# A ninth eighth in the first-stage buffer, another order of two interleaved transforms, and a half-size table of turns

## The chip, the cores and the metric

The kernel runs on one core of one Trainium2 chip. The time is device microseconds of one launch; the time before is the median of 10 runs, 204.54 us (203.83 to 204.83). One further execution was recorded by the hardware profiler; its times are microseconds from the start of its span.

The engines are named as in the profile: PE is TensorE's matmuls, PEld its weight loads, DVE is VectorE, ACT is ScalarE, POOL is GpSimd, SP is SyncE, which here only issues DMAs.

## The reference, cut to what matters

The sequence has 2048 positions, 512 channels and a batch of one; all tensors are bf16.

```python
def _A_ref(q, k, v, shift_k, ssm_k, ssm_D):
    # k_shift: four taps along the sequence
    for t in range(ks):
        k_shift = k_shift + k_pad[:, t:t + S, :] * shift_k[:, ks - 1 - t][None, None, :]
    kv = k_shift * v
    L = 2 * S
    kv_f = rfft2(kv_pad)          # along the sequence, zero padded to 4096
    kf_f = rfft2(kf_pad)          # ssm_k, the same
    y_f = kv_f * kf_f
    y = irfft2(y_f)[:S]
    y = y + kv * ssm_D
    return q * y

x = A_q
h = x + _A_ref(_layernorm(x), A_k, A_v, A_shift_k, A_ssm_k, A_ssm_D)
return h + _B_ref(_layernorm(h), B_w1, B_w2)      # B: relu(x @ w1) @ w2, 1376 wide
```

So there is a long convolution of kv with ssm_k, done by Fourier transforms, with a layer norm and a gate around it, and then an MLP.

## The kernel before

The transforms are written as matmuls with tables of sines and cosines. A transform of 4096 points is done in two stages: a first stage over short columns (`stage1`, 32 or 64 rows at a time against small bf16 tables) and a second stage (`stage2`, 128 by 128 tables `cc`, `cs` and `cn` in fp32r, one set for each of 32 odd frequencies k1). The tables are made on the chip: DVE computes turns as integers (`cs_turns`, `cc_turns`, `wrap`), ACT takes the sine (`table`, L193), and POOL makes the negated copy (`negated`, L250). The cosine's turns are the sine's plus a quarter (L222), wrapped (L189). Instructions are issued by hand in program order on each engine (`manual_schedule`), so the order of the Python code is the order on every queue; semaphores follow from which memory is written and read.

The stages that matter here, in order:

- **Loads and ssm_k to rows.** SP issues ssm_k, then k and v as four transposing loads each (L115 to L118). `to_rows` transposes ssm_k on PE, eight groups of four, and ACT or DVE copies each out of PSUM.
- **ssm_k's first stage with the taps** (L377 to L383), eight steps `gb`. In each, `taps` forms kv for a piece of the sequence: PE multiplies the shifted k by diagonal matrices (L369), and DVE multiplies the result by v (L372). Then `stage1` writes ssm_k's first-stage result to `a1` through two double banks of PSUM, evicted by ACT alone in even steps and by ACT and DVE in odd ones (`copy`, L259 on ACT, L261 on DVE). Steps 0 to 5 end with one `cc_part()`, which is one table on ACT: two for the sine's second part, then four for the cosine, from turns in `tcs`, which hold all 32 frequencies.
- **kv to rows** (L403): eight groups again, with evictions by DVE, ACT, DVE, DVE, ACT, DVE, ACT, DVE (L284 on DVE, L290 on ACT, two copies each).
- **The interleaved loop** (L410 to L421), eight steps `k4`. In each, ssm_k's second stage makes four frequencies, first the real part (evicted by DVE with ssm_D added, L418), then the imaginary part (evicted by ACT, L420). After both, one group of kv's first stage is made: two double banks, one evicted by ACT, the other by DVE (in groups 2 and 5 by DVE and ACT in halves). `a1` is one buffer of 64 KB a partition for both: a group of kv is written over the eighth that ssm_k's step has just read.
- **The product loop** (L475), 16 steps. kv's second stage (`u`), the complex product with ssm_k's spectrum (ACT copies a part of `u` to `usb`, L448; DVE and POOL multiply, L452, into `t`), and two steps later (`finish`) sums by matmul (`psy`, L462) and evictions into `kf`.
- **The inverse transform**, layer norm, gate and MLP, which take the rest of the span.

PSUM is handed out by `place`: `ring` is a list of tags, the first is taken and put at the back. Each tag is one double bank, and a tile waits until the tile before it on the same tag has been evicted. In the interleaved loop there are four tags (0 to 2 in the pool psF, 3 in psX); the order of tags there is 1, 3, 2, 0, so the real part always uses 1, the imaginary part 3 and kv's group 2 and 0. After the loop both pools are closed, and the product's `u` and `psy` tiles take their banks.

SBUF is full: on the left lie consts, `slotA` (a1, later `ax`), `vp` and `early`, whose place `kf` takes later; on the right lie the tables, `kvp` (k's first tiles), whose place `xfl`, then `prod` (the product loop's `t` and `usb`) and then `late` take.

Of the kernel before, what the change touches and what calls it, by code (L numbers as in the profile page):

```python
# [13 lines left out]
I32 = mybir.dt.int32  # L14
# [42 lines left out]
def kernel(  # L57
# [45 lines left out]
    kT = [(kvp if c < 2 else early).tile([P, DC, CH + 16], BF16, name=f"kT{c}") for c in range(4)]  # L103
# [79 lines left out]
    tcs = early.tile([P, 32, 64], I32, name="w_tc")  # L183
# [32 lines left out]
    dsc = early.tile([P, 2, 64], F32, name="dm_f")  # L216
    cs_turns(*cs[1])
    cc_parts = [(cs[1], tsn, dp) for dp in range(2)] + [(p, tcs, dp) for p in cc for dp in range(2)]

    def cc_turns(a):  # L220
        part = tcs[:, a:a + 16, :]
        nc.vector.tensor_single_scalar(out=part, in_=tsn[:, a:a + 16, :], scalar=2048.0, op=ALU.add)  # L222
        wrap(part, 8192)
# [47 lines left out]
    def bank2(name):  # L271
        return place([P, 2, 512], F32, name)
# [70 lines left out]
    cc_turns(16)  # L343
    _sin(dsc[:], t3[:], 64)
# [4 lines left out]
    a1 = slotA.tile([P, 64 * 256], F32R, tag="A", name="a1")  # L349

    def a1k_of(gb):
        return a1[:].rearrange("p (c j) -> p c j", j=256)[:, :, 32 * gb:32 * gb + 32]

    def a1k(c):
        return a1[:, 256 * c:256 * c + 256]

    def a1x_of(gb):
        return a1[:, 2048 * gb:2048 * gb + 2048].rearrange("p (c j) -> p c j", j=32)

    def a1x(c):  # L360
        return a1[:].rearrange("p (b c j) -> p b c j", b=8, j=32)[:, :, c, :]
# [15 lines left out]
    for gb in range(8):  # L377
        taps(gb // 2, gb % 2)
        stage1(kfl, a1k_of, gb, ("AA", "AD")[gb % 2], pairs=(gb == 2))
        if gb < 6:  # L380
            cc_part()
        if gb == 1:
            negated(22, 32)  # L383
# [25 lines left out]
    dcol = dtab[:].rearrange("p g r -> p (g r)").unsqueeze(2).to_broadcast([P, 256, 4])  # L409
    for k4 in range(8):  # L410
        ks = slice(4 * k4, 4 * k4 + 4)
        for s in range(2):
            ps = bank2("ps2k")
            for h in range(2):
                stage2(ps[:, h, :].rearrange("p (k j) -> p k j", k=2), a1k, 2 * k4 + h, s)
            pj = ps[:].rearrange("p b (k j) -> p j (b k)", k=2)
            if s == 0:
                nc.vector.tensor_tensor(out=kf[:, 0, :, ks], in0=pj, in1=dcol, op=ALU.add)  # L418
            else:
                nc.scalar.copy(out=kf[:, 1, :, ks], in_=pj)  # L420
        stage1(xfl, a1x_of, k4, ("A", "DA" if k4 in (2, 5) else "D"))  # L421
# [17 lines left out]
    def product(kp):  # L439
# [3 lines left out]
        for s in range(2):  # L443
            u = psu.tile([P, 2, 256], F32, tag=f"u{s}", name=f"u{s}")
            stage2(u[:].rearrange("p k (b j) -> p k b j", b=8), a1x, kp, s)
            usb = prod.tile([P, 256 - NJ, 2], F32, tag=f"usb{s}", name=f"usb{s}", bufs=2)
            uj = u[:].rearrange("p k j -> p j k")
            nc.scalar.copy(out=usb[:], in_=uj[:, po, :])  # L448
            t = prod.tile([P, 2, 256, 2], F32R, tag=f"t{s}", name=f"t{s}")
            for eng, in0, j in ((nc.vector, uj[:, dv, :], dv), (nc.gpsimd, usb[:], po)):  # L450
                n = j.stop - j.start
                eng.tensor_tensor(out=t[:, :, j, :], in0=in0.unsqueeze(1).to_broadcast([P, 2, n, 2]),  # L452
                                  in1=kfr[:, :, j, ks], op=ALU.mult)
            ts.append(t)
# [30 lines left out]
    ax = slotA.tile([P, P, 2, 64], F32R, tag="A", name="ax")  # L485
# [35 lines left out]
    bd = [late.tile([P, 2, 8, DC, 32], F32R, name="bd0")]  # L521
# [322 lines left out]
```

## Time and profile before

| what | value |
|---|---|
| median of 10 runs | 204.54 us |
| the profiled execution | 204.73 us |
| its span | 202.6 us |
| PE busy | 191.5 us (95%), 2337 matmuls |
| DVE busy | 145.0 us (72%) |
| ACT busy | 128.7 us (64%) |
| POOL busy | 85.5 us (42%) |
| granted TensorE clock | 1.00 over the span |

The span is what the profiler records from the first to the last instruction; the rest of the execution's time lies around it. Busy time of PE is modelled and overlaps from one matmul to the next, so a PE at 95% is not 95% of its peak; what counts is where it waits. A line of the timeline gives start, length, engine, line, operation, output and inputs, and in brackets how long the engine was idle before it and which instruction released it.

The stages lie in the span as follows: ssm_k's first stage with the taps until 35.4 us, kv to rows until 39.05, the interleaved loop until 60.4, the product loop until about 92.5, the inverse transform until 115, the MLP until the end.

### The profile page before, as it was taken

How to read it: one execution, taken by the hardware profiler on the slowest of the kernel's cores; microseconds unless marked ns; L12 is line 12 of the kernel's file. 1: busy time of each engine (PE TensorE's matmuls, PEld its weight loads, DVE VectorE, ACT ScalarE, POOL GpSimd, SP SyncE). 2: the span in 40 equal slices, each digit the busy share in tenths (PEclk: the TensorE clock that was granted, in tenths of full speed). 3: DMA queues.
4: the chain of work that ended last, by engine and by line, in shares of the span. 5: the costliest groups of instructions: out<-in, count | busy, mean ns of one | idle time of the engine just before them, and what ended most of it. 6: DMA issues, size and time to landing. Idle time of an engine off the chain costs nothing.

```text
span 202.6 us, 5574 instructions
## 1 busy us (share of the span) xinstructions
PE 191.5 (95%) x2337; PEld 135.3 (67%) x2337; DVE 145.0 (72%) x238; ACT 128.7 (64%) x199; POOL 85.5 (42%) x121
## 2 busy tenths in 40 slices
PE   7797979999997999999999999999999999999991
PEld 2473544999986989987998877545664556544451
DVE  7988767887877998988995698959477117662131
ACT  2668898778785888885979964924570583026300
POOL 7199995000006999995959384200120002002000
PEclk9999999999999999999999999999999999999999
DMA  6999992000000006819990979754481602160011
GB/s 185 332 218 146 180 161 58 3 5 3 3 3 5 0 3 184 263 42 227 234 234 15 110 92 186 140 104 106 88 155 50 110 0 52 32 97 29 0 52 52
DMA packets 48492, 20.06 MB, mean 99 GB/s; under 512 B 43380, under 2 KB 46932, under 8 KB 48468
## 3 DMA queue, kind: packets, MB, share of 16 engines
q1 hardware_dynamic: 47940, 19.71, 48.5%
q8 instruction: 18, 0.29, 0.6%
q10 hardware_dynamic: 528, 0.00, 0.1%
q14 instruction: 6, 0.05, 0.1%
HBM read 7.08 MB, written 2.10 MB: 45 GB/s over the span
## 4 chain that ended last, share of the span: by engine, by line
PE 69%; SPq 11%; DVE 8%; DMA 5%; ACT 3%; issue 1%; POOL 1%; ACTq 0%
PE ps1m L716 19%; PE ps2m L746 19%; PE psy L462 6%; PE ps2k L328 4%; SPq L118 4%; SPq L115 4%; PE ps2k L330 4%; PE u L328 4%; PE u L330 3%; DMA kT<-in_A_k_dram 3%; SPq L117 3%; PE pz L689 3%; PE ps L310 2%; PE pst L281 2%; PE pkv L369 2%; DVE st L547 2%
## 5 line engine op out<-in xcount | busy, mean ns | idle before, releaser
L731 ACT ACTIVATE h1T<-ps1m 128x512 bf16<-128x512 f32 (+1 forms) x44 | 25.7, 597 | 35.8 <-PE ps1m L716 35.7
L716 PE MATMUL ps1m<-xT,w 128*128 128x512 bf16 (+2 forms) x192 | 43.7, 365 | 0.4 <-DVE xT L662 0.4
L746 PE MATMUL ps2m<-w,h1T 128*128 128x512 bf16 (+3 forms) x187 | 40.8, 368 | 0.0
L689 PE MATMUL pz<-bd,ax 128*128 128x128 f32 x96 | 35.7, 410 | 0.0
L452 POOL TENSOR_TENSOR t<-usb,kf 128x320 fp32r<-128x320 f32 x32 | 28.2, 911 | 2.2 <-ACT usb L448 1.7
L452 DVE TENSOR_TENSOR t<-u,kf 128x704 fp32r<-128x704 f32 x32 | 26.7, 885 | 3.2 <-ACT usb L448 3.2
L750 DVE SCALAR_TENSOR_TENSOR o<-ps2m,rstd,xh 128x512 bf16<-128x512 f32 (+1 forms) x17 | 12.1, 717 | 22.5 <-PE ps2m L746 11.5
L746 PEld LDWEIGHTS <-h1T 128*128 128x128 bf16 (+1 forms) x187 | 16.2, 98 | 16.0
L553 POOL TENSOR_SCALAR rstd<-mv 128x4 f32<-128x4 f32 x8 | 2.5, 316 | 57.0 <-DVE mv L551 57.0
L259 ACT CAST a<-ps 128x1024 fp32r<-128x1024 f32 (+1 forms) x22 | 22.5, 1056 | 4.0 <-PE ps L310 3.9
L716 PEld LDWEIGHTS <-w 128*128 128x128 bf16 (+1 forms) x192 | 15.9, 100 | 12.1 <-DVE xT L662 0.5
L689 PEld LDWEIGHTS pz<-bd,ax 128*128 128x128 f32 x96 | 18.6, 193 | 7.6
L547 DVE BATCH_NORM_STATS2 st<-xh 128x6 f32<-128x512 bf16 x32 | 19.9, 679 | 0.4 <-DMA xh<-xT 0.4
L660 DVE TENSOR_TENSOR qT<-pz,qT 128x1024 bf16<-128x1024 f32 x8 | 9.8, 1220 | 13.5 <-PE pz L689 10.8
L259 ACT CAST kf<-psy 128x512 fp32r<-128x512 f32 x30 | 17.5, 644 | 1.9 <-PE psy L462 0.2
L537 ACT ACTIVATE bd<-ecw,nbias 32x512 fp32r<-32x512 int32 x24 | 17.3, 720 | 0.6
L369 PE MATMUL pkv<-kT,wdiag 128*128 128x512 bf16 x64 | 15.2, 380 | 2.2 <-POOL f_hi L247 1.1
L462 PE MATMUL psy<-t,ipos 128*128 128x512 f32 x48 | 16.0, 394 | 0.0
L261 DVE CAST a<-ps 128x1024 fp32r<-128x1024 f32 (+1 forms) x12 | 13.6, 1137 | 2.7 <-PE ps L310 2.6
L259 ACT CAST ax<-psi 128x1024 fp32r<-128x1024 f32 x13 | 12.3, 1040 | 3.7 <-PE psi L609 3.5
L372 DVE TENSOR_TENSOR sk<-pkv,vT 128x512 bf16<-128x512 f32 x16 | 10.7, 689 | 5.2 <-PE pkv L369 3.5
L609 PE MATMUL psi<-dre,kf 64*128 64x128 f32 x120 | 13.8, 275 | 0.1
(132 smaller groups left out, 399.2 us busy)
## 6 DMA issues: line engine op xcount, KB each, us to landing
sk<-in_A_ssm_k_dram SPq DMA_DIRECT2D x1, 2048.0 KB
xh<-in_A_q_dram SPq DMA_DIRECT2D x16, 128.0 KB
out_dram<-o SPq DMA_DIRECT2D x15, 128.0 KB
w<-in_B_w_dram SPq DMA_DIRECT2D x1, 1376.0 KB
w<-in_B_w_dram SPq DMA_DIRECT2D x1, 1280.0 KB
xh<-xT SPq DMA_TRANSPOSE x8
out_dram<-o SPq DMA_DIRECT2D x2, 64.0 KB
w<-in_B_w_dram SPq DMA_DIRECT2D x1, 96.0 KB
```

What stands on the lines that cost most here:

```text
L259: nc.scalar.copy(out=o, in_=i)
L328: nc.tensor.matmul(out=ps[:, kk, :], lhsT=at_k1(w_re, k1), rhs=a_in(2 * k1), start=True, stop=False, skip_group_check=True)
L330: nc.tensor.matmul(out=ps[:, kk, :], lhsT=at_k1(w_im, k1), rhs=a_in(2 * k1 + 1), start=False, stop=True, skip_group_check=True)
L369: nc.tensor.matmul(out=pss[i][:], lhsT=wdiag[:, 2 * h + i, j, :], rhs=kT[c][:, 2 * h + i, 16 - j:CH + 16 - j], start=(j == 0), stop=(j == ...
L452: eng.tensor_tensor(out=t[:, :, j, :], in0=in0.unsqueeze(1).to_broadcast([P, 2, n, 2]), in1=kfr[:, :, j, ks], op=ALU.mult)
L462: nc.tensor.matmul(out=psy[:], lhsT=m_[:], rhs=t_.rearrange("p j k -> p (j k)"), start=first, stop=not first)
L537: nc.scalar.activation(out=bd[h][rows, :, :, rg, :], in_=ecw[q % 2][rows, :, 256 * h:256 * h + 256].rearrange("p b (j n) -> p b j n", n=32 ...
L547: nc.vector.bn_stats(out=st[:, i, :], in_=src[:, i, :])
L689: nc.tensor.matmul(out=pz[:, il, :, a, :], lhsT=ax[:, 64 * rho + n2, :, :].rearrange("p d g -> p (d g)"), rhs=bd[h][:, rho, 4 * il + a, :, ...
L716: nc.tensor.matmul(out=ps1[fc][:fsz, 128 * ii.start:128 * ii.stop].rearrange("p (i t) -> p i t", t=P), lhsT=w1[:, c, fc * P:fc * P + fsz], ...
L731: nc.scalar.activation(out=h1T[:fsz, fc, :], in_=ps1[fc][:fsz, :], func=ACT.Relu)
L746: nc.tensor.matmul(out=ps2[:, 0:w], lhsT=h1T[:ksz, fc, i * P:(i + 1) * P], rhs=w2[:ksz, fc, ds], start=(fc == 0), stop=(fc == NFC - 1))
```

## The change

- `a1` gets nine eighths instead of eight and is allocated earlier. ssm_k's first-stage result lies in eighths 1 to 8, kv's groups go to eighths 0 to 7. Group 0 of kv has a place of its own, and group g may be written once ssm_k's step g-1 has read its eighth.
- The interleaved loop runs in another order. Step 0 is as before: real, imaginary, group 0. In step 1 group 1 stands between the real and the imaginary part, and group 2 after it. From step 2 on group k4+1 follows step k4, so that group 7 is made in step 6 and step 7 ends with ssm_k's imaginary part. The ring starts as 1, 0, 2, 3.
- The turns of the cosine, `tcs`, have room for 16 frequencies instead of 32. The second half is made in step 4 of ssm_k's first stage, in place of a table; the two tables that use it come in steps 5 and 6 instead of 4 and 5.
- The products' second buffer `t1` lies, for two steps out of three, in the ninth eighth of `a1`, which nothing reads any more; the pool keeps one buffer for the third.
- `bd0`, a table of the inverse transform, moves from `late` into the ninth eighth.
- k's third tile moves from `early` to `kvp`, and the sine `dsc` is taken in place.

```diff
--- before.py
+++ after.py
@@ -100,7 +100,7 @@
     draw = consts.tile([P, DC, 64], BF16, name="draw")
     vT = [vp.tile([P, DC, 512], BF16, name=f"vT{c}") for c in range(4)]
     CH = 512
-    kT = [(kvp if c < 2 else early).tile([P, DC, CH + 16], BF16, name=f"kT{c}") for c in range(4)]
+    kT = [(kvp if c < 3 else early).tile([P, DC, CH + 16], BF16, name=f"kT{c}") for c in range(4)]
     wdiag = kvp.tile([P, DC, KS, P], BF16, name="wdiag")
 
     idle = vT[3][:, 0, :]
@@ -180,7 +180,9 @@
         return t[:, k1 - a, :]
 
     tsn = early.tile([P, 32, 64], I32, name="w_ts")
-    tcs = early.tile([P, 32, 64], I32, name="w_tc")
+    tcs = early.tile([P, 16, 64], I32, name="w_tc")
+    EIGHTH = 64 * 32
+    a1 = slotA.tile([P, 9 * EIGHTH], F32R, tag="A", name="a1")
     ta = early.tile([P, 96], F32, name="w_ta")
     nc.vector.tensor_scalar(out=ta[:, 0:32], in0=r2[:, 0:32], scalar1=n2c[:], scalar2=4096.0, op0=ALU.mult, op1=ALU.add)
     nc.vector.tensor_scalar(out=ta[:, 32:96], in0=r2[:, 32:96], scalar1=n2c[:], scalar2=0.0, op0=ALU.mult, op1=ALU.add)
@@ -213,12 +215,12 @@
     t3 = early.tile([P, 2, 64], I32, name="dm_t")
     _turns(nc, t3[:, 0, :], r2[:, 32:96], n2s[:], 64, True)
     _turns(nc, t3[:, 1, :], r2[:, 32:96], n2s[:], 64, False)
-    dsc = early.tile([P, 2, 64], F32, name="dm_f")
+    dsc = t3[:].bitcast(F32)
     cs_turns(*cs[1])
-    cc_parts = [(cs[1], tsn, dp) for dp in range(2)] + [(p, tcs, dp) for p in cc for dp in range(2)]
+    cc_parts = [(cs[1], tsn, dp) for dp in range(2)] + [((0, p[1]), tcs, dp) for p in cc for dp in range(2)]
 
     def cc_turns(a):
-        part = tcs[:, a:a + 16, :]
+        part = tcs[:]
         nc.vector.tensor_single_scalar(out=part, in_=tsn[:, a:a + 16, :], scalar=2048.0, op=ALU.add)
         wrap(part, 8192)
 
@@ -340,25 +342,23 @@
 
     for q in range(8):
         to_rows(sk_word, q, kfl, "DADDADAD"[q])
-    cc_turns(16)
-    _sin(dsc[:], t3[:], 64)
+    _sin(dsc, t3[:], 64)
     dre = consts.tile([P, 2, 2, 64], F32R, name="dre")
     dim = consts.tile([P, 2, 2, 64], F32R, name="dim")
     nc.gpsimd.memset(dre[:].bitcast(F32), 0.0)
     nc.gpsimd.memset(dim[:].bitcast(F32), 0.0)
-    a1 = slotA.tile([P, 64 * 256], F32R, tag="A", name="a1")
 
     def a1k_of(gb):
-        return a1[:].rearrange("p (c j) -> p c j", j=256)[:, :, 32 * gb:32 * gb + 32]
+        return a1[:, EIGHTH:].rearrange("p (c j) -> p c j", j=256)[:, :, 32 * gb:32 * gb + 32]
 
     def a1k(c):
-        return a1[:, 256 * c:256 * c + 256]
+        return a1[:, EIGHTH + 256 * c:EIGHTH + 256 * c + 256]
 
     def a1x_of(gb):
-        return a1[:, 2048 * gb:2048 * gb + 2048].rearrange("p (c j) -> p c j", j=32)
+        return a1[:, EIGHTH * gb:EIGHTH * gb + EIGHTH].rearrange("p (c j) -> p c j", j=32)
 
     def a1x(c):
-        return a1[:].rearrange("p (b c j) -> p b c j", b=8, j=32)[:, :, c, :]
+        return a1[:, 0:8 * EIGHTH].rearrange("p (b c j) -> p b c j", b=8, j=32)[:, :, c, :]
 
 
     kvp2 = sk[:].rearrange("p c t -> p (c t)").rearrange("p (m c a e) -> p m c a e", m=32, c=DC, e=2)
@@ -377,7 +377,9 @@
     for gb in range(8):
         taps(gb // 2, gb % 2)
         stage1(kfl, a1k_of, gb, ("AA", "AD")[gb % 2], pairs=(gb == 2))
-        if gb < 6:
+        if gb == 4:
+            cc_turns(16)
+        elif gb < 7:
             cc_part()
         if gb == 1:
             negated(22, 32)
@@ -407,18 +409,29 @@
     slotB = pl.push("slotB")
     kf = slotB.tile([P, 2, 256, 32], F32R, tag="B", name="kf")
     dcol = dtab[:].rearrange("p g r -> p (g r)").unsqueeze(2).to_broadcast([P, 256, 4])
+
+    def spectrum_k(k4, s):
+        ks = slice(4 * k4, 4 * k4 + 4)
+        ps = bank2("ps2k")
+        for h in range(2):
+            stage2(ps[:, h, :].rearrange("p (k j) -> p k j", k=2), a1k, 2 * k4 + h, s)
+        pj = ps[:].rearrange("p b (k j) -> p j (b k)", k=2)
+        if s == 0:
+            nc.vector.tensor_tensor(out=kf[:, 0, :, ks], in0=pj, in1=dcol, op=ALU.add)
+        else:
+            nc.scalar.copy(out=kf[:, 1, :, ks], in_=pj)
+
+    def rows_kv(gb):
+        stage1(xfl, a1x_of, gb, ("A", "DA" if gb in (2, 5) else "D"))
+
+    ring[:] = [1, 0, 2, 3]
     for k4 in range(8):
-        ks = slice(4 * k4, 4 * k4 + 4)
-        for s in range(2):
-            ps = bank2("ps2k")
-            for h in range(2):
-                stage2(ps[:, h, :].rearrange("p (k j) -> p k j", k=2), a1k, 2 * k4 + h, s)
-            pj = ps[:].rearrange("p b (k j) -> p j (b k)", k=2)
-            if s == 0:
-                nc.vector.tensor_tensor(out=kf[:, 0, :, ks], in0=pj, in1=dcol, op=ALU.add)
-            else:
-                nc.scalar.copy(out=kf[:, 1, :, ks], in_=pj)
-        stage1(xfl, a1x_of, k4, ("A", "DA" if k4 in (2, 5) else "D"))
+        spectrum_k(k4, 0)
+        if k4 == 1:
+            rows_kv(1)
+        spectrum_k(k4, 1)
+        if k4 < 7:
+            rows_kv(k4 + 1 if k4 else 0)
     pl.pop("psX")
     pl.pop("psF")
     pl.pop("xfp")
@@ -446,7 +459,11 @@
             usb = prod.tile([P, 256 - NJ, 2], F32, tag=f"usb{s}", name=f"usb{s}", bufs=2)
             uj = u[:].rearrange("p k j -> p j k")
             nc.scalar.copy(out=usb[:], in_=uj[:, po, :])
-            t = prod.tile([P, 2, 256, 2], F32R, tag=f"t{s}", name=f"t{s}")
+            if s == 1 and kp % 3 < 2:
+                at = 8 * EIGHTH + 1024 * (kp % 3)
+                t = a1[:, at:at + 1024].rearrange("p (c j k) -> p c j k", c=2, k=2)
+            else:
+                t = prod.tile([P, 2, 256, 2], F32R, tag=f"t{s}", name=f"t{s}", bufs=3 - 2 * s)[:]
             for eng, in0, j in ((nc.vector, uj[:, dv, :], dv), (nc.gpsimd, usb[:], po)):
                 n = j.stop - j.start
                 eng.tensor_tensor(out=t[:, :, j, :], in0=in0.unsqueeze(1).to_broadcast([P, 2, n, 2]),
@@ -482,7 +499,8 @@
         if kp == 10:
             w1 = wp.tile([P, DC, DFF], BF16, tag="c2s0", name="w1")
             nc.sync.dma_start(out=w1[:], in_=B_w1.rearrange("(c p) f -> p c f", p=P))
-    ax = slotA.tile([P, P, 2, 64], F32R, tag="A", name="ax")
+    ax_bd = slotA.tile([P, 9 * EIGHTH], F32R, tag="A", name="ax")
+    ax = ax_bd[:, 0:8 * EIGHTH].rearrange("p (x d g) -> p x d g", x=P, d=2)
     load_x(2)
     load_x(3)
     pl.pop("psU")
@@ -518,7 +536,7 @@
     ecw = [late.tile([P, 2, 512], I32, name="ecw0"), wp.tile([P, 2, 512], I32, tag="c2s1", name="ecw1")]
     ecore0 = wp.tile([P, 2, 16, 32], F32R, tag="c2n0", name="ecore0")
     w2 = wp.tile([P, NFC, D], BF16, tag="c2n1", name="w2")
-    bd = [late.tile([P, 2, 8, DC, 32], F32R, name="bd0")]
+    bd = [ax_bd[:, 8 * EIGHTH:].rearrange("p (b j r n) -> p b j r n", b=2, j=8, r=DC)]
     act_pool = {0: late}
 
     def ec_turns(q):
```

## The prediction, made before the run

> **What bounds the kernel now.** I read three views in this order: the stretches of the span by engine, the chain of waits, and the timeline of each engine around the lines that the diff touches. The stretches (start:end, length, then busy us and instruction count of PE, PEld, DVE, ACT and POOL, the granted clock, DMA share, GB/s):
>
> ```profile
> 35.40:39.05 3.65, 3.65 (x32) 3.38 (x32) 3.50 (x5) 3.10 (x6) 0.00 (x0) 1.00 0.02 4
> 39.05:60.40 21.35, 21.35 (x642) 19.97 (x640) 17.65 (x17) 16.55 (x19) 0.00 (x0) 1.00 0.02 3
> 60.40:64.80 4.40, 2.89 (x28) 2.50 (x20) 2.95 (x4) 2.64 (x6) 2.47 (x4) 1.00 0.02 6
> 64.80:92.50 27.70, 27.68 (x172) 24.76 (x172) 25.50 (x31) 23.66 (x58) 26.53 (x31) 1.00 0.35 102
> ```
>
> TensorE (PE) sets the pace from 35.4 us on, at full clock. The interleaved loop (ssm_k's second step, kv's first) fills 21.35 of 21.35 us, the product loop 27.68 of 27.70. Between them lies one hole, and the timeline shows what it is made of (start, length, engine):
>
> ```profile
> 59.88 1.01 ACT L420 CAST kf<-ps2k 128x1024 fp32r<-128x1024 f32 x1 [0.70 <-PE ps2k L330]
> 60.79 1.08 ACT L259 CAST a<-ps 128x1024 fp32r<-128x1024 f32 x1
> 61.93 0.38 PE L328 MATMUL u<-a,c2c 128*128 128x256 f32 x1 [1.48 <-ACT a L259]
> 62.75 0.73 ACT L448 COPY usb<-u 128x160 f32<-128x160 f32 x2 [0.88 <-PE u L330]
> 63.08 1.69 DVE L452 TENSOR_TENSOR t<-u,kf 128x704 fp32r<-128x704 f32 x2 [1.29 <-ACT usb L448]
> ```
>
> PE idles 1.48 us because the first product reads what kv's last group (I write r7) has just left in PSUM, and its eviction on ACT queues behind ssm_k's. This is what the reordering aims at. Ahead of 35.4 us the chain of waits runs through the transposing loads on SP's queue: kT's last load is issued at 23.48 and lands at 30.10.
>
> **The change, part by part.** I write s0(k), s1(k) for the two halves of ssm_k's step k, r(g) for kv's group g.
>
> **1. The hole goes: -1.15.** Let F be the first matmul of s1(7), 58.74 in the PE timeline. Before, the first product on DVE starts at 63.08 = F+4.34. After, r7 is done one step earlier. ACT's copy of s1(7) starts F+1.14 (59.88), ACT takes its next work 0.91 later (60.79), so usb starts at F+2.05, and DVE follows it by 0.33 (63.08-62.75): F+2.38. PE's first product matmuls come at F+0.91 and usb could follow 0.82 after that (62.75-61.93), so ACT is what is late. That is 1.96 gained; but F now has r7 ahead of it, which costs PE 0.62 (a group, 41.08 to 41.72 less jitter) and 0.19 for the turn from wide to narrow matmuls (1.10 from s1 to a group, 0.91 from s0 to s1). Net 1.15, not 1.48: the hole is not filled but exchanged for ACT's 1.01 copy.
>
> **2. The cosine turns in halves push a table: +0.60.** With one half-size buffer, step 4 of ssm_k's first stage gives up its table to make the second half of the turns, and the last two tables (L193) move to steps 5 and 6. Nothing was behind step 6 on ACT before:
>
> ```profile
> 25.70 1.27 ACT L193 ACTIVATE c2c<-w_tc,hbi,hsc 128x1024 fp32r<-128x1024 int32 x1
> 26.84 2.06 ACT L259 CAST a<-ps 128x1024 fp32r<-128x1024 f32 x2
> ...
> 31.05 1.23 ACT L193 ACTIVATE c2c<-w_tc,hbi,hsc 128x1024 fp32r<-128x1024 int32 x1
> 32.73 2.04 ACT L259 CAST a<-ps 128x1024 fp32r<-128x1024 f32 x2 [0.44 <-PE ps L310]
> 35.17 1.13 ACT L259 CAST a<-ps 128x1024 fp32r<-128x1024 f32 x1 [0.41 <-PE ps L310]
> ...
> 36.36 0.96 PEld L281 LDWEIGHTS pst<-ident,sk 128*128 128x128 f32 x9 [0.16 <-ACT a L259]
> ...
> 36.36 3.62 DVE L284 TENSOR_SCALAR xfl<-pst 128x512 int32<-128x512 int32 x5
> ```
>
> The pair at 32.73 is step 6, the single at 35.17 step 7. A table delays the next copy by 1.14 (25.70 to 26.84), so with one between them step 7's copy starts at 34.65+1.14 = 35.79 instead of 35.17. The third kv transpose group (36.36) waits for exactly that PSUM bank: 35.17+1.13+0.06. So it moves 0.6, and with it DVE's dense row of five copies and s0(0), PE having no slack from there on. Step 4 without its table saves nothing: ACT idles 0.44 and 0.41 before steps 6 and 7 already. What is late next: s1(0) takes, by the new ring, the bank that DVE empties last (39.98 before), +0.04.
>
> **3. Two groups close together: +0.80.** The new order begins s0(0) s1(0) r0 s0(1) r1 s1(1) r2, over four double banks. r1 needs the bank of r0's half that ACT evicts, and ACT first copies s1(0):
>
> ```profile
> 41.31 1.01 ACT L420 CAST kf<-ps2k 128x1024 fp32r<-128x1024 f32 x1 [1.33 <-issue]
> 42.22 1.10 ACT L259 CAST a<-ps 128x1024 fp32r<-128x1024 f32 x1
> ```
>
> With r0's first matmul at R = 41.08 that bank is free at 43.32 = R+2.24 (+0.06 to the matmul); PE wants r1 at R+0.62+1.10 = R+1.72. Stall 0.55 (rounded down for jitter). Then r2 needs the bank of r1's ACT half: copy begins 0.80 after r1's first matmul (as DVE's at 41.92 does after 41.08), lasts 1.10, free 1.96 after; wanted at 1.72: 0.25. From r3 on a whole s0, s1 pair lies between groups and the rotation is the old one, where PE never waited.
>
> **4. The moved turns on DVE: 0 to +0.92, I take +0.15.** Two instructions (L222, L189) leave DVE at 13.52 and come back after step 4's products, at 27.89. Leaving gives nothing: PE waits for kT's load until 30.10. At 27.89 they stand ahead of step 5's two products (L372), which free the bank that PE's next taps need at 30.14. They are 0.69 each, but GpSimd is in the way:
>
> ```profile
> 12.35 2.04 POOL L238 TENSOR_TENSOR wdiag<-ident,wsh 128x512 bf16<-128x512 bf16 x2
> 14.33 1.99 POOL L247 COPY f_hi<-f_hi 32x64 bf16<-32x64 bf16 x4
> 25.64 3.45 POOL L250 TENSOR_SCALAR c2n<-c2s 128x1280 fp32r<-128x1280 f32 x1
> ...
> 13.52 1.42 DVE L222 TENSOR_SCALAR w_tc<-w_ts 128x1024 int32<-128x1024 int32 x1
> 14.97 0.69 DVE L189 TENSOR_SCALAR w_tc<-w_tc 128x1024 int32<-128x1024 int32 x1
> ```
>
> L222 alone took 0.69 at 8.21; here it took 1.42 and ended 0.55 after POOL's instruction did (14.39 to 14.94), while POOL's four copies then took 1.99 where the like four took 1.06. If POOL stays where it is, L250 ends at 29.09, L222 at 29.64, L189 at 30.33, the product after it at 31.0: PE is 0.92 late. But with L222 gone from 13.52, POOL's copies run 0.93 earlier and all behind them: L250 ends at 28.16, L222 at 28.71, L189 at 29.40, the product at 30.05, in time for 30.14. I take a value near this end, since the queue of POOL is unbroken from 12.35 to 29.
>
> The Trainium skill (SBUF — State Buffer, section "SBUF: two separate sides") says that VectorE's two-port modes and GpSimd take one shared port pair in turns, for a whole instruction. By it the turns are blocked until L250 ends, which is what I reckoned from the rows; the rows of 0.69 alone, without it, would make this term 0.
>
> **5. At nothing.** The products' buffers keep number, shape and strides (two of three in the ninth eighth): no new wait while the last s1 reads of that eighth precede them on PE. The sine table in place, kT's third tile in another pool and the offset of a1 change addresses only. bd0 moves into the ninth eighth; its memset (1.80, at 100.55 on POOL) comes after the last product matmul (92.73) as before, with 8 us until its first use at 110.32. No DMA is added or dropped; SP's x load waits for the last product and moves with it.
>
> **Sum.** -1.15+0.60+0.04+0.80+0.15 = +0.44 at the first product, and the product loop without slack hands it on whole; what waits later (x load, statistics, MLP) hangs from its end. The profiled execution took 204.73 (span 202.6 and 2.1 around it), 0.19 above the median: 205.17 in its terms, 204.54+0.44 = 205.0 in the median's. I forecast slightly slower. A difference under 0.2% (0.41 us) is about what a measurement of this kernel can't tell from no change, so this is on the edge.
>
> **Rivals.** (a) The late table is free: if transposes were not bound to that bank, part 2 falls away, -0.16 in all: 204.4. For it: ACT idles near there; against it: the wait at 36.36 names this very copy. (b) Faster: the close groups cost nothing, PE being fed through other banks while ACT catches up; +0.44-0.80 = -0.36: 204.2. It decides if ACT's copy of r0 ends within R+1.66; against it stands R+2.24. (c) POOL does not move up: part 4 costs 0.92: 205.75. Against: the unbroken queue. (d) The change doesn't do what it says: the product's PSUM pool waits for all evictions of the pool before it, s1(7)'s among them. Then PE starts at F+1.14+1.01+0.06, usb 0.82 later, DVE at F+3.36: gain 0.17 instead of 1.15: 206.0. The trace before can't tell, as there the same copy held data and bank.
>
> **How the numbers follow.** Forecast 0.58, of which slower 0.37, same 0.21 (its own range 204.7 to 205.4: jitter of 0.1 in four stalls, half of part 4); (a) 0.17, same 0.09, faster 0.08; (b) 0.14, faster 0.12, same 0.02; (c) 0.06 and (d) 0.05, slower. Faster 0.20, same 0.32, slower 0.48. The range 204.1 to 205.75 takes in (a), (b) and the upper end of part 4, and leaves out (d) and (a) with (b) together.
>
> **What would show it.** Part 1: the first u matmul follows s1(7) without a wait, and DVE's first product follows ACT's L420 copy by some 1.2 us. Part 2: a c2c table on ACT between step 6 and step 7, and the third transpose group later by 0.6. Part 3: two PE waits on ACT a L259 in the first three steps. Part 4: L222 near 27.9 lasting longer than 0.69. I am wrong if the first product on DVE is not between 63.2 and 63.9, or if the product loop or the MLP changes its length.

## The result, and the profile after

| what | before | after |
|---|---|---|
| median | 204.52 us (32 runs, 203.78 to 204.83) | 205.44 us (9 runs, 205.38 to 205.97) |
| ratio of after to before | | 1.0052, 95% interval 1.0042 to 1.0062 |
| profiled execution, its span | 204.73, 202.6 | 205.76, 204.0 |
| time outside the span, median of the runs | 2.14 | 1.78 |
| first matmul of the interleaved loop | 39.05 | 39.58 |
| first product on DVE | 63.08 | 64.27 |
| first pz matmul (inverse, second stage) | 110.69 | 111.72 |
| first gate instruction on DVE | 112.94 | 114.34 |
| first MLP matmul | 114.95 | 116.34 |

The kernel became slower by 0.92 us; 0.44 was forecast (205.0, within 204.1 to 205.75). Read down the table, the span's 1.39 is lost in three places: 0.53 before the interleaved loop, 0.66 in it and in the turn to the products, and 0.37 between pz and the gate; the product loop with the inverse transform gives 0.16 back. The time grew by less than the span, because what lies around the span is 0.36 shorter. It is shorter in every kernel that has the change (1.78 to 1.87 against 2.14); the runs do not show why.

The first view is PE's list of waits after the change (who waited for whom: us in all, times, longest); these are the lines that are new from 36 us on:

```profile
PE u L330 <- DVE kf L420: 0.6, 1, 0.6
PE pst L283 <- ACT a L261: 0.5, 1, 0.5
PE ps L312 <- ACT a L261: 0.3, 1, 0.3
PE ps2k L332 <- issue: 0.3, 1, 0.3
```

The old hole, 1.5 us at `u` for ACT's copy of kv's last group, is gone. Two of the four waits were forecast: `pst` (the late table) and `ps` (two groups close together). Two were not: the first product matmul waits for DVE, and in ssm_k's third step PE stands still for no semaphore at all ("issue"). The timeline shows the close groups and the stall in the third step:

```profile
43.45 0.20 PE L312 MATMUL ps<-f_hi,xfl 32*128 32x64 bf16 x2
43.98 0.20 PE L312 MATMUL ps<-f_hi,xfl 32*128 32x64 bf16 x2 [0.33 <-ACT a L261]
...
47.07 0.28 PE L330 MATMUL ps2k<-a,c2c 128*128 128x256 f32 x1
47.68 0.38 PE L332 MATMUL ps2k<-a,c2s 128*128 128x256 f32 x1 [0.33 <-issue]
```

Next the table on ACT between step 6 (the pair) and step 7 (the single copy), and PE behind it:

```profile
32.71 2.05 ACT L261 CAST a<-ps 128x1024 fp32r<-128x1024 f32 x2 [0.78 <-PE ps L312]
34.65 1.23 ACT L195 ACTIVATE c2c<-w_tc,hbi,hsc 128x1024 fp32r<-128x1024 int32 x1
35.78 1.05 ACT L261 CAST a<-ps 128x1024 fp32r<-128x1024 f32 x1
...
36.88 2.84 PE L283 MATMUL pst<-ident,sk 128*128 128x128 f32 x24 [0.46 <-ACT a L261]
```

From step 6's first copy to step 7's it is 3.07, against 2.44 before (32.73 to 35.17), and kv's third transpose group starts at 36.88 instead of 36.36. Last the turn to the products:

```profile
61.78 1.22 DVE L420 TENSOR_TENSOR kf<-ps2k,dtab 128x1024 fp32r<-128x1024 f32 x1
...
62.60 1.01 ACT L422 CAST kf<-ps2k 128x1024 fp32r<-128x1024 f32 x1 [0.64 <-PE ps2k L332]
63.15 0.36 PE L330 MATMUL u<-a,c2c 128*128 128x256 f32 x1 [0.58 <-DVE kf L420]
63.95 0.73 ACT L461 COPY usb<-u 128x160 f32<-128x160 f32 x2 [0.33 <-PE u L332]
64.27 0.89 DVE L469 TENSOR_TENSOR t<-u,kf 128x704 fp32r<-128x704 f32 x1 [1.27 <-ACT usb L461]
```

kv's group 7 was done long ago, but PE starts `u` only when DVE has evicted ssm_k's last real part (61.78 + 1.22). In the program `u` lies in other banks than that; what it waits for is the closing of the pool psF, of which the real part's bank is one. So ACT, free at 63.61 after the last imaginary part, idles 0.33 more, and DVE's first product comes 2.78 after the first matmul of s1(7) (61.49), not 2.38.

### The profile page after: what moved, and what is told of

It reads as the page before. It is cut to its first block, busy times and chain, and to the rows that moved or that the text cites. A ratio compares the mean times of both kernels' runs of the same rounds, so it can differ in the third digit from the quotient of the medians.

```text
span 204.0 us, 5565 instructions
## 1 busy us (share of the span) xinstructions
PE 193.3 (95%) x2337; PEld 136.0 (67%) x2337; DVE 144.5 (71%) x238; ACT 128.4 (63%) x199; POOL 85.6 (42%) x121
## 4 chain that ended last, share of the span: by engine, by line
PE 67%; DVE 11%; SPq 9%; DMA 5%; ACT 4%; issue 2%; POOL 1%; ACTq 0%; DVEq 0%
PE ps1m L734 19%; PE ps2m L764 19%; PE psy L479 6%; SPq L115 4%; PE u L330 4%; DMA vT<-in_A_v_dram 3%; PE ps2k L330 3%; PE u L332 3%; SPq L117 3%; PE pz L707 3%; PE ps2k L332 3%; PE ps L312 3%; SPq L118 2%; PE pst L283 2%; PE pkv L369 2%
## 5 line engine op out<-in xcount | busy, mean ns | idle before, releaser
L469 POOL TENSOR_TENSOR t<-usb,kf 128x320 fp32r<-128x320 f32 x21 | 19.2, 942 | 3.0 <-ACT usb L461 2.6
L469 DVE TENSOR_TENSOR t<-u,kf 128x704 fp32r<-128x704 f32 x21 | 18.2, 888 | 3.0 <-ACT usb L461 2.7
L678 DVE TENSOR_TENSOR qT<-pz,qT 128x1024 bf16<-128x1024 f32 x8 | 9.8, 1220 | 14.0 <-PE pz L707 10.8
L707 PE MATMUL pz<-ax 128*128 128x128 f32 x48 | 17.9, 410 | 0.0
L707 PE MATMUL pz<-bd,ax 128*128 128x128 f32 x48 | 17.8, 410 | 0.0
L627 PE MATMUL psi<-dim,kf 64*128 64x128 f32 x120 | 13.6, 270 | 0.0
L479 PE MATMUL psy<-t,ipos 128*128 128x512 f32 x37 | 13.5, 392 | 0.0
```

Of the source, the lines that this page charges most:

```text
L479: nc.tensor.matmul(out=psy[:], lhsT=m_[:], rhs=t_.rearrange("p j k -> p (j k)"), start=first, stop=not first)
L627: nc.tensor.matmul(out=banks[dp][:, 128 * i:128 * i + 128], lhsT=kf[halves[dp], c, 4 * m:4 * m + 4, :].rearrange("p r k -> p (r k)"), rhs= ...
L707: nc.tensor.matmul(out=pz[:, il, :, a, :], lhsT=ax[:, 64 * rho + n2, :, :].rearrange("p d g -> p (d g)"), rhs=bd[h][:, rho, 4 * il + a, :, ...
```

## The experiments

Each kernel was compared with the kernel before on the same chip; the medians of the kernel before there were 204.54 to 204.73. Times of different rows are compared through the ratio. Line numbers of variants can differ by up to five.

**The changed kernel once more.**

> The changed kernel once more, unaltered. Time 205.3 to 205.6. It tells which of the new idle stretches belong to the program. If the stall of 0.5 us in the middle of ssm_k's third step (a wait that the trace puts down to issue) and the extra 0.37 us between the product loop's end and the gate are properties of the program, both come again at the same instructions, within 0.1 us; if they are chance of one execution, at least one of them is gone and the span is shorter by its size. The late table (third group of kv's transposes at 36.9), the wait of kv's group 1 (0.5) and the wait of the first u matmul (0.58) hang from the order alone and must come again under every theory.

205.62 us, ratio 1.0036 (1.0021 to 1.0051). Every wait from kv's transposes on came again, at the same instruction and within 0.1: the stall without a semaphore at 47.63 (47.68 before), the gate 2.63 after pz (2.62). They belong to the program.

**The table in step 5 instead of after step 6.**

```diff
         if gb == 4:
             cc_turns(16)
-        elif gb < 7:
+        elif gb < 6:
             cc_part()
+            if gb == 5:
+                cc_part()
```

> The changed kernel with its last cosine table made in step 5 beside the one there, none after step 6. My theory (the late table holds ACT's copy of step 7, hence the bank of the third transpose group, hence everything): the third transpose group goes back from 36.9 to 36.4, the first matmul of the interleaved loop from 39.6 to 39.05, and the time falls by 0.5, to 204.9. Rival (the late table is covered, the changed kernel loses elsewhere): time unchanged at 205.4. Second rival (two tables in a row delay step 5's or step 6's evictions instead, by 1.1 less the idle time of 0.4 before each): the gain is smaller than 0.2 or turns into a loss.

205.15 us, ratio 1.0026 (1.0009 to 1.0043): 0.47 less than the changed kernel beside it by the medians. The two intervals overlap, so the size rests on the trace: the interleaved loop's first matmul is at 39.15, not 39.58. From step 6's copy to step 7's it is 2.45 again, and the transposes run without the gap. Two tables in a row in step 5 cost at most 0.13 (step 6's copy at 32.83, not 32.70), so the second rival is out.

**The kernel before with the late table alone.**

```diff
-        if gb < 6:
+        if gb < 7 and gb != 4:
             cc_part()
```

> The kernel before, with nothing changed but the place of its tables: none in step 4 of ssm_k's first stage, the last two in steps 5 and 6 (the turns are still made whole). My theory: the table after step 6 delays ACT's copy of step 7 by 0.6, the third group of kv's transposes with it, and the time by 0.5, to 205.1, although the old order of the interleaved loop and its hole before the first product are kept. Rival (the table is only late because the changed kernel's turns come late): no change, 204.6.

205.10 us beside 204.73, ratio 1.0023 (1.0001 to 1.0045): slower by 0.4, with an interval that just leaves out no change. On ACT (its timeline):

```profile
32.01 2.02 ACT L259 CAST a<-ps 128x1024 fp32r<-128x1024 f32 x2 [0.49 <-PE ps L310]
33.90 1.25 ACT L193 ACTIVATE c2c<-w_tc,hbi,hsc 128x1024 fp32r<-128x1024 int32 x1
35.27 1.16 ACT L259 CAST a<-ps 128x1024 fp32r<-128x1024 f32 x1
```

It is 3.26 from step 6 to step 7, but not by the table: that ended at 35.15, and the copy at 35.27 came when PE had step 7's matmuls done (35.29 by its signal). In this execution kT's last load landed early and step 6 with it (PE's taps for it at 29.03, not 30.14), while step 7's taps began at 32.70, behind DVE, which had waited for a load of v until 31.95. So this profile, with the old span of 202.6, does not show the table's cost; the profiled execution took 204.70, the least of its twelve, and the 0.4 is shown by the medians alone.

**The third double bank in a pool of its own.**

```diff
+    psum2 = pl.push("psG", space=PSUM)
...
-    places = [psum] * 3
+    places = [psum, psum, psum2]
...
+    pl.pop("psG")
     pl.pop("psF")
```

> The changed kernel with the third double bank of the interleaved loop in a PSUM pool of its own, closed one pool apart from the two others, so that the first u matmul waits for kv's group 7 alone and not for DVE's eviction of ssm_k's last real part. My theory (closing a pool makes the first tile behind it wait for the last eviction of the whole pool): the wait of 0.58 before the first u matmul goes, the first copy into usb follows ACT's copy of the last imaginary part, DVE's first product starts 0.4 earlier, time 205.0. Rival (ACT's copy is what is late anyway): the wait goes and the time stays at 205.4.

205.29 us, ratio 1.0023 (1.0008 to 1.0038), 0.33 less. The timeline:

```profile
62.15 0.28 PE L331 MATMUL u<-a,c2c 128*128 128x256 f32 x1
...
62.34 1.02 ACT L423 CAST kf<-ps2k 128x1024 fp32r<-128x1024 f32 x1 [0.69 <-PE ps2k L333]
...
63.26 0.82 ACT L463 COPY usb<-u 128x160 f32<-128x160 f32 x3
...
63.59 0.89 DVE L471 TENSOR_TENSOR t<-u,kf 128x704 fp32r<-128x704 f32 x1 [0.90 <-ACT usb L463]
```

`u` follows s1(7) without a gap, ACT goes straight from `kf` to `usb`, and DVE starts 2.39 after s1(7)'s first matmul (61.20): the 2.38 of the prediction. Closing the pool as a whole cost 0.40.

**Groups further apart.** On top of the split pool:

```diff
-    ring[:] = [1, 0, 2, 3]
+    ring[:] = [1, 0, 3, 2]
     for k4 in range(8):
         spectrum_k(k4, 0)
-        if k4 == 1:
-            rows_kv(1)
+        if k4 < 2:
+            rows_kv(k4)
         spectrum_k(k4, 1)
-        if k4 < 7:
-            rows_kv(k4 + 1 if k4 else 0)
+        if 0 < k4 < 7:
+            rows_kv(k4 + 1)
```

> The one before with the order of the first three steps also changed: kv's groups 0, 1 and 2 each get one half of ssm_k's step more between them (real, group 0, imaginary, real, group 1, imaginary, group 2), and the ring starts 1, 0, 3, 2. My theory (groups 1 and 2 wait for the bank that ACT evicts, since two groups follow each other with one half between them): group 1 has no wait, group 2 one of 0.25 or less, 0.5 less than the kernel with the split pool alone: 204.5. Rival (the close groups cost nothing, as PE is late for another reason): same time as the kernel with the split pool alone.

204.59 us, ratio 0.9995 (0.9977 to 1.0012): 0.7 less than the split alone, and the kernel before's time. The bank wait of group 1 is gone from PE's list; the stall without a semaphore grew:

```profile
PE ps2k L333 <- issue: 0.5, 1, 0.5
PE pst L284 <- ACT a L262: 0.5, 1, 0.5
PE u L331 <- DVE t L471: 0.3, 1, 0.3
```

In the profile 0.35 lies ahead of the loop (its first matmul at 39.21, not 39.56; GpSimd was through with L252 before DVE's turns began). From there to DVE's first product it is only 0.16 shorter, 23.87 against 24.03: what the bank waits gave back went to the stall, which grew from 0.35 between two matmuls to 0.79. So the loop alone does not explain the 0.7 of the medians; nothing that was edited lies ahead of the loop, and the rest stays open.

**Every group between the two halves of its step.** On top of the split pool, the real part's bank now being the one in psG:

```diff
-    places = [psum, psum, psum2]
+    places = [psum, psum2, psum]
...
-    ring[:] = [1, 0, 2, 3]
+    ring[:] = [1, 2, 0, 3]
     for k4 in range(8):
         spectrum_k(k4, 0)
-        if k4 == 1:
-            rows_kv(1)
+        rows_kv(k4)
         spectrum_k(k4, 1)
-        if k4 < 7:
-            rows_kv(k4 + 1 if k4 else 0)
```

> The changed kernel with the split pool, and with every group of kv between the real and the imaginary part of its own step, so that two halves of ssm_k's step lie between any two groups. Against the spread order (where three groups of 64 narrow matmuls still follow within 5 us and PE idles 0.65 in ssm_k's third step without a semaphore). Theory A (PE runs out of instructions where narrow matmuls are dense): that idle time goes, the turn to the products costs 0.1 more, time 204.1. Theory B (the idle time belongs to that place, whatever comes before): it stays, time 204.6 to 204.7.

205.33 us, ratio 1.0027 (1.0010 to 1.0043). A miss twice over. Its list of waits:

```profile
PE u L331 <- DVE a L264: 0.8, 1, 0.8
PE ps L313 <- issue: 0.5, 1, 0.5
```

I had put the turn to the products at 0.1 and overlooked that DVE then evicts s0(7) and group 7 one after the other (60.41 and 61.55, 1.22 each). And the stall did not go with the dense groups: it is there, in the middle of a group of kv. Theory A in that form fell, but so did B, since it is another place in the work. What the two have in common shows when PE's instructions up to the stall are counted. From the view of stretches, first the changed kernel, then this one (start:end, length, busy us and count of PE and PEld):

```profile
0.00:47.60 47.60, 42.79 (x859) 27.12 (x859) 37.22 (x67) 34.35 (x41) 27.21 (x55) 1.00 0.73 137
```

```profile
0.00:47.15 47.15, 41.91 (x859) 26.90 (x859) 37.27 (x67) 33.73 (x40) 27.18 (x55) 1.00 0.73 138
```

859 weight loads in both, and 859 in the spread order too (0 to 46.85). PE stops (from 47.07 to 47.68 after the change, from 46.53 to 47.21 here) at one point of its stream of instructions, whatever work stands there. The DMA of the same stretches fits: nothing of the kernel is transferred there, yet there is traffic (last column, GB/s). Before:

```profile
43.00:44.40 1.40, 1.40 (x73) 1.23 (x71) 1.28 (x2) 0.87 (x2) 0.00 (x0) 1.00 0.08 18
44.40:46.40 2.00, 2.00 (x20) 1.91 (x16) 1.86 (x2) 1.46 (x2) 0.00 (x0) 1.00 0.00 0
```

After:

```profile
43.00:44.40 1.40, 1.07 (x63) 0.83 (x62) 1.40 (x2) 0.93 (x1) 0.00 (x0) 1.00 0.00 0
44.40:46.40 2.00, 1.99 (x101) 1.72 (x88) 1.57 (x2) 1.65 (x2) 0.00 (x0) 1.00 0.05 12
46.40:48.00 1.60, 1.27 (x28) 1.03 (x16) 0.69 (x1) 1.60 (x3) 0.00 (x0) 1.00 0.00 0
```

18 GB/s over 1.40 us are 25 KB, as are 12 over 2.00; the page lists two queues of kind "instruction" with 18 and 6 packets (0.29 and 0.05 MB, so 16 KB and 8 KB each). The piece that came between 43.0 and 44.4 before comes after 44.4 now. The fit is a loose one: after the change the traffic is over by 46.40, and PE stops only after 47.07.

**The same work in more instructions.** The warming matmuls at the start, ahead of everything, were cut smaller, in the changed kernel alone and in the best one (below):

```diff
-    for _ in range(22):
-        nc.tensor.matmul(out=warm[:], lhsT=idle[:, 0:P], rhs=idle, start=True, stop=True)
+    for _ in range(44):
+        nc.tensor.matmul(out=warm[:, 0:256], lhsT=idle[:, 0:P], rhs=idle[:, 0:256], start=True, stop=True)
```

> The changed kernel with nothing altered but its warming matmuls: 44 of 256 columns in place of 22 of 512, so that 22 matmuls and weight loads more stand ahead in PE's stream. If the idle time in ssm_k's third step (0.45 to 0.5 beyond the usual spacing) is a matter of where PE's stream of instructions is cut, it goes as it did in the kernel with the spread order, the stretch from the first matmul of the interleaved loop to DVE's first product shrinks from 24.6 to 24.15, and the time falls to 205.0 to 205.1; the bank waits of group 1 and of the first u matmul stay. If the reordered loop brings the idle time with it wherever the stream is cut, both stay at 24.6 and 205.5.

> The one before, with the warming matmuls at the start as 44 of 256 columns in place of 22 of 512: the same work and time on PE, but 22 matmuls and as many weight loads more in its stream of instructions. Theory A (PE's idle time in the third step is its supply of instructions: it stood at the 859th matmul in three different orders): the idle time moves by some 22 matmuls in the work, or changes its length, or is gone (then 203.2 to 203.4). Theory B (it belongs to the place in the work): again 0.65 at the sixth matmul of ssm_k's third real part, same time as the one before.

> The same with 88 warming matmuls of 128 columns: 66 matmuls and weight loads more ahead. Theory A: the idle time moves by some 66 matmuls, to before or into ssm_k's second step, or is gone (203.2 to 203.4). Theory B: no change against the one with 22.

The kernels with 44 and 88 pieces in the best one took 203.84 (ratio 0.9961, 0.9944 to 0.9978) and 203.69 (0.9967, 0.9947 to 0.9987). In all three the stall in the third step is gone. In two of them, though, PE now stands still earlier, as the lists from 10 to 75 us show, first the changed kernel with 44 pieces, then the best one with 88:

```profile
PE pkv L369 <- issue: 0.6, 1, 0.6
PE u L330 <- DVE kf L420: 0.5, 1, 0.5
...
PE pst L283 <- ACT a L261: 0.4, 1, 0.4
...
PE ps L312 <- ACT a L261: 0.3, 1, 0.3
```

```profile
PE ps L313 <- issue: 0.9, 1, 0.9
```

These stalls end at 19.21 and 29.63, and 221 and 477 weight loads stand ahead of them, against 859 ahead of the old one. With the matmuls and the waits counted that is 448, 960 and 1728 instructions: the places lie 512 and 768 apart, both multiples of 256. The kernel with the late table alone has a short stall at 960 as well (0.24 idle, at 31.40). So the stall depends on the place in PE's stream and not on the work that stands there, as theory A says.

From the loop's first matmul to DVE's first product it takes 24.00 (24.69 and 24.59 in the changed kernel's two profiles), in the best kernel 23.23 and 23.24 instead of 23.71, but there the loop begins later, at 39.42 and 39.22 instead of 39.03. That the stall is PE's supply of instructions is shown by where it stands. That it is worth its 0.5 in the time is not: the medians are 205.69 (ratio 1.0049, 1.0030 to 1.0069) for the changed kernel, and, for the best, 203.84 and 203.69 against 203.70. The profiled execution of the first was the fastest of its six, 204.64, the others took 205.27 to 205.99. Nor do the runs say why the piece comes later in the new order.

**GpSimd's zeroing and the gate.** First the zeroing of `bd1` moved to VectorE:

```diff
-    nc.gpsimd.memset(bd[1][:].bitcast(F32), 0.0)
+    nc.vector.memset(bd[1][:].bitcast(F32), 0.0)
```

> The changed kernel with the second table of the inverse transform (bd1) zeroed by VectorE instead of GpSimd; the rest unaltered. In the changed kernel and its four variants the first gate instruction on VectorE starts 2.62 after the first pz matmul, in the kernel before 2.25; GpSimd's zeroing ends within 0.03 of the moment at which PE is done, and the fourth sine into bd0 ends just as the gate starts. Theory A (VectorE has to wait behind GpSimd at the moment of the zeroing's end): the gate starts 2.25 after the first pz matmul, time 205.1. Theory B (the gate waits for the four sines, because bd0 now lies in one buffer with the inverse transform's operand): it stays at 2.62, time 205.5.

205.41 us, ratio 1.0040 (1.0019 to 1.0062). The gate starts right behind the zeroing, at 113.92, 2.46 after the first pz matmul, while the fourth sine into `bd0` runs until 114.06: it does not wait for the sines, so theory B fell. Theory A is not shown by it, since the zeroing (1.76 on DVE) itself ends after PE. And the MLP loses 0.4 (88.06 from its first matmul to the end, against 87.63), with another stall on issue at 117.35, ahead of which 3776 instructions stand on PE: 2048 more than ahead of the stall in the loop. Nothing is gained.

**All edits with the even order.**

> The changed kernel with all of it: both last tables in step 5, the split pool, every group of kv between the two parts of its own step, bd1 zeroed by VectorE. The costs that the runs before showed add up: 0.5 for the table, 0.4 for the pool, 0.55 for the close groups' bank waits, 0.5 for the idle time in the third step, 0.37 for the gate if it was GpSimd's doing. If all of them are terms of one sum, 203.2; without the last two, 204.0; if the gains overlap (one wait taking the other's place), 204.3 or more.

204.60 us, ratio 0.9995 (0.9977 to 1.0013). The gains did not add up: the even order gave back at `u`, and the MLP was longer by 0.4 as in the run before, with its stall on issue at the same place in PE's stream.

**The spread order, the table in step 5, and the zeroing split over both engines.**

```diff
-    nc.gpsimd.memset(bd[1][:].bitcast(F32), 0.0)
+    nc.gpsimd.memset(bd[1][:, 0].bitcast(F32), 0.0)
+    nc.vector.memset(bd[1][:, 1].bitcast(F32), 0.0)
```

> The spread order with the split pool, and with two edits more: both last tables in step 5, and bd1 zeroed half by GpSimd, half by VectorE, so that neither is at it when PE has finished the first half of pz. Against the spread kernel alone: 0.47 from the table, and the gate 2.25 after the first pz matmul in place of 2.62 if GpSimd's zeroing was what held VectorE (0.37, or 0.2 if something else is late next): 203.8 to 203.9. If the gate's delay is of another kind, 2.62 stays and the time is 204.1. PE's idle time of 0.65 in ssm_k's third step stays in any case.

203.70 us, ratio 0.9953 (0.9938 to 0.9968): with its two variants above the fastest of the study, and faster than both kernels. The gate, first before the change, then after it, then here (timelines of PE, POOL and DVE):

```profile
110.69 3.86 PE L677 MATMUL pz<-ecore,ax 32*128 32x256 f32 x128 [0.22 <-DVE ax L261]
...
111.15 1.80 POOL L652 MEMSET bd<- 128x2048 f32 x1
...
112.94 1.22 DVE L660 TENSOR_TENSOR qT<-pz,qT 128x1024 bf16<-128x1024 f32 x1 [1.86 <-ACT bd L537]
```

```profile
111.72 3.87 PE L695 MATMUL pz<-ecore,ax 32*128 32x256 f32 x128 [0.22 <-DVE ax L263]
...
112.19 1.80 POOL L670 MEMSET bd<- 128x2048 f32 x1
...
114.34 1.23 DVE L678 TENSOR_TENSOR qT<-pz,qT 128x1024 bf16<-128x1024 f32 x1 [2.22 <-ACT ax L555]
```

```profile
110.18 3.87 PE L700 MATMUL pz<-ecore,ax 32*128 32x256 f32 x128 [0.22 <-DVE ax L264]
...
110.65 0.95 POOL L674 MEMSET bd<- 128x1024 f32 x1
...
112.45 1.23 DVE L683 TENSOR_TENSOR qT<-pz,qT 128x1024 bf16<-128x1024 f32 x1 [0.80 <-ACT ax L559]
```

It is 2.27 instead of 2.62, so the edit removes the gate's 0.35. That GpSimd's zeroing is what held DVE does not follow. Before the change the same zeroing ended at the same moment, 2.26 after the first pz matmul (2.27 after the change), and the gate began there without a delay. The waits that DVE's queue carries out tell more (view of one line: count, shortest, middle and longest ns, first and last start). Before the change, after it, and here:

```profile
L660 DVEq EVENT_SEMAPHORE  x2: 21/1165/2309, 110.5 to 110.6; - x2
L662 DVEq EVENT_SEMAPHORE  x1: 21/21/21, 113.4 to 113.4; - x1
```

```profile
L678 DVEq EVENT_SEMAPHORE  x2: 21/1168/2315, 111.6 to 111.6; - x2
L680 DVEq EVENT_SEMAPHORE  x1: 21/21/21, 114.4 to 114.4; - x1
```

```profile
L683 DVEq EVENT_SEMAPHORE  x2: 21/981/1941, 110.0 to 110.5; - x2
```

The two waits of L660, L678 and L683 stand ahead of the gate, the one of L662 and L680 behind it. Before the change the wait behind the gate comes 0.41 after the gate's start. After the change it comes 0.04 after it, and it is the gate that comes 0.40 after the wait for PE is over (113.94). Here the second wait comes 0.42 after the first, where the other two kernels have 0.05. So one step of DVE's queue is some 0.4 late in each kernel, and counted along the queue it is the same one: after the change one more instruction stands ahead of the gate than before, and with a zeroing on DVE two more. All fourteen profiles have it there, 0.40 to 0.42 late. Before the change it fell behind the gate, after the change on the gate, and here on a wait for PE that lasts until 112.40 anyway. By these traces the gate's 0.35 belongs to DVE's supply of instructions, and the added zeroing moved it; no run added an instruction without a zeroing, and why that step is late they do not show.

Not tried: the change with turns at full size, SBUF being full.

## Why the prediction was right, and where its sum was not

The direction was right and the time lies in the range; the sum was half of what was measured, and terms of it stood at nothing that are not nothing. One of its own signs of being wrong came true: the first product came at 64.27, not between 63.2 and 63.9. And the time has luck in it: the prediction carried the 2.1 around the span over, which became 1.78. With 2.14 around the changed kernel's median span of 203.7 it would be 205.8 (an estimate from these two numbers), just above the range.

- **Part 1, -1.15.** The hole went and ACT's copy of s1(7) became what is late, as forecast. The size fell short by 0.40, so the term is -0.75: rival (d) is right in its mechanism (the pool waits as a whole) with another member of the pool, DVE's eviction of s0(7) instead of ACT's of s1(7), which lies in psX. I had weighed the pool only against the copy that carried data and bank before. The split pool gave 2.39 against the reckoned 2.38.
- **Part 2, +0.60.** Right: 3.07 against 2.44 on ACT, 0.52 on the transposes, 0.47 in the medians when taken back, 0.4 in the medians when added to the old kernel. Rival (a) is out.
- **Part 3, +0.55 and +0.25.** Right. Group 1's third matmul was due at 43.46, right behind the first two as in other groups, and came at 43.98, 0.52 late; group 2 lost 0.2. In the spread order group 1's wait is gone. Rival (b) is out.
- **Part 4, +0.15.** GpSimd moved up as reckoned (`f_hi`'s four copies 1.07 together, not 1.99), and L224 ended at 28.74 (28.71 was reckoned). PE's next taps began at 30.14, as before: cost 0 between these two profiles, and rival (c) is out. But it is 0 only beside a late load. Before, PE waited there for kT; after, for DVE (0.48), and when the loads landed early, in the repeated run, it waited 1.37 for DVE and began at 30.13 all the same.
- **Part 5, at nothing.** This is the step that failed. That buffers keep their number and no DMA is added says nothing of the supply of instructions, on PE (0.49 in the third step: 0.61 between two matmuls that are 0.12 apart elsewhere) or on DVE at the gate (0.37), although no line there was changed. A wait of the gate for GpSimd or for the sines into `bd0`, which the change did move, is out by the traces above.

At the first product these make -0.75 + 0.52 + 0.52 + 0.20 + 0.49 = +0.98; measured is +1.19, so 0.21 in small pieces is not assigned. The 0.16 that the product loop and the inverse transform gave back were not looked into.

The shared port of part 4 is better shown than in the old kernel. On DVE, L224 in the changed kernel, and in its repetition (timeline of DVE); GpSimd's L252 ends at 28.18 and 28.17:

```profile
27.62 1.12 DVE L224 TENSOR_SCALAR w_tc<-w_ts 128x1024 int32<-128x1024 int32 x1
```

```profile
26.71 2.00 DVE L224 TENSOR_SCALAR w_tc<-w_ts 128x1024 int32<-128x1024 int32 x1
```

Started 0.91 apart, they end at 28.74 and 28.71; where GpSimd had ended before the start (the spread order) it takes 0.69. The Trainium skill (SBUF — State Buffer, section "SBUF: two separate sides") has the pair of ports held for a whole instruction, and these rows agree: L224 ends 0.56 and 0.54 after L252, however early it began.

## What to carry to other kernels

A stall that is removed is worth what the next one leaves, so ask of every resource that the new order touches what else hangs on it: a PSUM pool closes as a whole, and one bank evicted late holds the first tile behind it; a pool for each moment of release cost three lines and gave 0.4 in the trace, 0.33 in the medians. Before a step is put later on an engine, look for the copy behind it and count its idle time; put the step where the idle time is. When an engine is late for no semaphore, count the instructions ahead of it before blaming a neighbour that happens to end then, and look at the same place in the old kernel. And compare stages, not spans: step 6's first copy on ACT started anywhere from 32.0 to 33.7 in these profiles, which is more than all that was studied.

## What the runs showed of the hardware that was not expected

PE can stand still for lack of instructions. In the trace it is an idle time of PE whose releaser is "issue". Nine profiles have it after 859 weight loads, in three orders of the work (0.23 beyond the usual spacing with the split pool, 0.73 with all edits). With 22 or 66 matmuls more ahead it left that place, and in two of three kernels it stood at another. Ahead of all these stalls stand 448, 960, 1728 or 3776 instructions, which are 512, 768 and 2048 apart. The page's 18 pieces of 16 KB fit this: PE's 2337 matmuls, as many weight loads and some 40 waits make one piece for about 260 instructions (an estimate from these counts, if that queue is PE's). At most such places nothing is lost: the kernel before has no stall at any of them.

DVE's queue has one late step of the same kind, 0.40 to 0.42 in all fourteen profiles. What it costs depends on what stands there: nothing before the change, 0.37 when it fell on the gate.
